# Score, projection, FFN and output products in tiles of 64x64 instead of 64x32, beside P.V in 64x32

## The chip, the cores and the metric

The kernel runs on one core of one Trainium2 chip. The metric is the device time of one execution in microseconds (us); the median of several runs counts. TensorE multiplies, VectorE (DVE), ScalarE (ACT) and GpSimd (POOL) work on the results, and SyncE (SP) issues most of the DMAs. On TensorE each product is two instructions: a load of the stationary operand (the profile calls this queue PEld) and the matmul that streams the moving operand past it (PE).

## The reference

One input `x` of 2048 tokens by 512 features goes through an attention block (32 heads of 16) and through a gated FFN of width 1376; a sigmoid gate mixes the two. All inputs are bf16.

```python
    qkv = (x @ wqkv)                       # q, k, v: 32 heads, Dh = 16
    scores = jnp.einsum("bhqd,bhkd->bhqk", q, k) * (Dh ** -0.5)
    p = _softmax(scores, axis=-1)
    o = jnp.einsum("bhqk,bhkd->bhqd", p, v)
    a = o_merged @ wo
    ...
    g_ = jnp.einsum("bsd,df->bsf", x, w_gate)
    u = jnp.einsum("bsd,df->bsf", x, w_up)
    b = jnp.einsum("bsf,fd->bsd", g_ * u, w_down)
    ...
    g = _sigmoid((x * gate_w).sum(-1, keepdims=True))
    return g * a + (1 - g) * b
```

(Names are shortened here; the shapes are those of the reference.)

## The kernel before

**Halves and tiles.** After a short prologue TensorE is used as two halves of 64 rows, `r = 0` and `r = 1`. One job is what a half does at once: a product of 64 contraction rows with up to 128 output columns and 512 moving columns, written as matmuls side by side, each at its own place in the array. `pe64` (line 1570) issues such a list; `tile_position=(64 * r, 32 * cc)` names the half and the column where a matmul's tile begins. In the kernel before, every job is four matmuls of 64 rows by 32 columns, so eight tiles cover the array when both halves work. The shape of a tile in the built program follows from the operands: rows and output columns, rounded up to 32, 64 or 128.

**Which jobs there are.** `scores` (line 1579) makes the scores of 128 keys by 512 queries for one head: the stationary operand is a slice of the keys `KT`, the moving one the masked queries `QM`. `fill` (line 1607) makes one contraction step of everything that is a plain matrix product: the k, q and v projections, the FFN's up and gate products (`u`, `g`), the FFN's down product together with the output projection (`do`), the last chunk's output projection (`fin`), and the row of the gate (one column wide). `pv` (line 1595) makes P.V: four heads in one job, each with its own 17 columns (16 of V and one of ones, which gives the softmax's denominator) and its own moving operand, so that these are four matmuls in four 32-column places by nature. `tail_out` makes the last output products, again with four matmuls a job. The only full-array matmuls are those of the prologue (7 warm-up matmuls, 16 transposes, 32 projections) and `x_turn` (line 1651), four calls of four transposes each near the beginning.

**What the other engines do.** ACT takes the exponential of part of the score tiles out of PSUM, up to three banks in one instruction. For the other part DVE forms the exponential as an integer pass over the scores' bits, and DVE and GpSimd (`int64_add`) make three shifted copies of it, which P.V then reads with scaled copies `Vs` of V. DVE also copies projections, multiplies up by gate, and scales outputs.

**What sets the order.** A planner (`_Sched`) runs when the program is built: an event loop with a clock, assumed durations (0.216 us for a job on one half), tables of limits by time, and pools of PSUM banks and SBUF cells. At each step it picks for each half the next job: P.V on one half (`vh`), scores and filling products on the other, mostly in turn. Each pick becomes one call of `scores`, `pv` or `fill`, which appends one operation to the plan; `emit` then writes each engine's list in that order and adds the semaphore waits that the operands need. An operation's wait stands at its first matmul, and its signal at its last. The number of matmuls inside a job is not known to the planner: neither the choice nor the order of jobs depends on it.

Of the kernel before, what the change touches and what calls it, by code (L numbers as in the profile page):

```python
# [1502 lines left out]
class _Hw:  # L1503
# [63 lines left out]
        self.ps = stack.enter_context(nc.psum_tensor("ps", [128, 8, 512], F32))  # L1567


    def pe64(self, r, mms, deps):  # L1570
        def fn(pe):
            o = None
            for dst, lhs, rhs, st, sp, cc in mms:
                o = pe.matmul(dst, lhs, rhs, start=st, stop=sp, tile_position=(64 * r, 32 * cc), skip_group_check=True)  # L1574
            return o

        return self.P.op("pe", fn, deps, "pe%d" % r)

    def scores(self, r, bank, c, b, s, kt, ci, deps):
        var = s + 2 * (ci % 2)  # L1580
        lo, hi = 64 * r, 64 * r + 64
        q = self.QM[lo:hi, (4 * c + b) % 2, var, :]
        mms = []
        for cc in range(4):
            k0 = kt * 128 + 32 * cc
            mms.append((self.ps[32 * cc : 32 * cc + 32, bank, :], self.KT[lo:hi, b, k0 : k0 + 32], q, True, True, cc))
        return self.pe64(r, mms, deps)

    def cell(self, x, lo, hi):
# [17 lines left out]
    def fill(self, u, r, i, start, stop, deps):  # L1607
        lo, hi = 64 * r, 64 * r + 64
        bank = u.bank
        kind = u.mm[0]  # L1610
        mms = []
        n = 4
        if kind == "gate":
            for cc in range(1, 4) if u.mm[1] else (0,):
                mms.append((self.ps[32 * cc : 32 * cc + 1, bank, :], self.gw[lo:hi, i : i + 1], self.xT[lo:hi, cc, i, :], start, stop, cc))
            return self.pe64(r, mms, deps)
        for cc in range(4):
            c0 = 32 * cc
            if kind in ("k", "q", "u", "g"):
                if kind == "k":  # L1620
                    b, ch = u.mm[1:]
                    w = self.wk[lo:hi, i, 128 * b + c0 : 128 * b + c0 + 32]
                elif kind == "q":
                    ch, b = u.mm[1:]
                    w = self.wq[lo:hi, i, 128 * b + c0 : 128 * b + c0 + 32]
                else:
                    ch, f = u.mm[1:]
                    if c0 >= self.FW[f]:
                        continue
                    w = (self.wu if kind == "u" else self.wg)[lo:hi, i, 128 * f + c0 : 128 * f + c0 + 32]  # L1630
                x = self.xT[lo:hi, ch, i, :]
            elif kind == "v":
                ch, tt = divmod(u.mm[1], 4)
                t0 = 128 * tt + c0
                w, x = self.xT[lo:hi, ch, i, t0 : t0 + 32], self.wv[lo:hi, i, :]
            elif kind == "do":
                c, tt = u.mm[1:]
                t0 = 128 * tt + c0
                if i < 11:
                    w, x = self.hT[lo:hi, i, t0 : t0 + 32], self.wd[lo:hi, i, :]  # L1640
                else:
                    w, x = self.OT[lo:hi, (4 * c + i - 11) % 8, t0 : t0 + 32], self.wo[lo:hi, i - 11, :]
            else:
                t0 = 128 * u.mm[1] + c0
                w = self.OT[lo:hi, (12 + i) % 8, t0 : t0 + 32]
                x = self.wo[lo:hi, i, :] if i < 3 else self.wq[lo:hi, 0, :]
            mms.append((self.ps[c0 : c0 + 32, bank, :], w, x, start, stop, cc))
        return self.pe64(r, mms, deps)


# [531 lines left out]
```

## Time and profile before

| | |
|---|---|
| median of 3 runs | 699.54 us |
| the runs | 699.54, 692.03, 699.86 us |
| the profiled execution | 705.51 us, span of its instructions 703.7 us |
| granted TensorE clock, mean | 0.997 |
| HBM read, written | 12.23 MB, 2.36 MB |

The page of the profile gives busy time and instruction count of each engine, the span in 40 slices, the chain of work that ended last, and the costliest groups of instructions. A row of a group names the line, the engine, the operation, output and inputs, the tile's rows and columns where it is a matmul (64*32), the operands' shapes and the count; then the busy time as a union, the mean length of one in ns, and the idle time before the group with what ended it. `issue` is time in which an engine waited for nothing that the profile shows. Lengths of matmuls are modelled; the distance between the starts of two matmuls on one tile says how long the tile is taken.

Busy time in two stretches of the span (PE, PEld, DVE, ACT, POOL in us):

| stretch | PE | PEld | DVE | ACT | POOL |
|---|---|---|---|---|---|
| 200 to 300 us | 99.24 | 58.62 | 87.95 | 98.07 | 89.96 |
| 690 to 704 us | 9.16 | 5.21 | 6.09 | 6.13 | 1.49 |

### The profile page before, as it was taken

What the parts mean: (1) busy time and instruction counts of PE and PEld (TensorE: products, weight loads), DVE (VectorE), ACT (ScalarE), POOL (GpSimd) and SP (SyncE); (2) the same over time, 40 slices, a digit from 0 to 9 for tenths busy, and PEclk for the clock granted to TensorE, in tenths of its full rate; (3) what the DMA queues carried; (4) which work ended last, traced back from release to release, by engine and by line L of the source; (5) the groups of instructions that cost most, each with busy time, mean ns of one, the idle gap of its engine ahead of it and who ended that gap; (6) DMA issues with size and microseconds to landing.
All of it is one profiled execution on the core that took longest, in us unless ns stands there. A gap on an engine that the chain in (4) does not pass through costs nothing.

```text
span 703.7 us, 49393 instructions
## 1 busy us (share of the span) xinstructions
PE 682.0 (97%) x22839; PEld 393.0 (56%) x22839; DVE 624.5 (89%) x1008; ACT 660.0 (94%) x1040; POOL 545.3 (77%) x617
## 2 busy tenths in 40 slices
PE   8999999999999999999997999999999999999997
PEld 5566555455465565555653566545554565556564
DVE  7889989899898879999998888999899878999985
ACT  5899999999899999999997999999999999999995
POOL 3455988788989889998997667879799877772790
PEclk9999999999999999999999999999999999999999
DMA  9101422001310010101010010100101010010101
GB/s 180 45 5 29 112 66 65 13 9 32 85 36 19 23 33 18 30 6 36 6 24 23 20 43 13 36 4 13 28 10 38 13 27 30 12 28 12 37 8 46
DMA packets 32126, 23.06 MB, mean 33 GB/s; under 512 B 17356, under 2 KB 28524, under 8 KB 31920
## 3 DMA queue, kind: packets, MB, share of 16 engines
q1 hardware_dynamic: 30784, 18.86, 10.6%
q8 instruction: 178, 2.92, 1.8%
q0 software_dynamic: 176, 0.53, 0.5%
q10 hardware_dynamic: 960, 0.52, 0.3%
q14 instruction: 28, 0.23, 0.1%
HBM read 12.23 MB, written 2.36 MB: 21 GB/s over the span
## 4 chain that ended last, share of the span: by engine, by line
PE 92%; DVE 4%; issue 2%; POOL 1%; ACT 0%; DVEq 0%; POOLq 0%; ACTq 0%
PE ps L1574 92%; DVE DB L1710 1%; DVE OT L1869 1%; POOL DB L1717 1%; PE ps L1978 0%; DVE io L1880 0%; ACT wu L1671 0%; PE ps L1963 0%; DVE hT L1848 0%; ACT wd L1671 0%; POOL wk L1717 0%; DVE wk L1710 0%; DVE gden L1697 0%; DVE ident L1885 0%; DVE qraw L1732 0%
## 5 line engine op out<-in xcount | busy, mean ns | idle before, releaser
L1574 PE MATMUL ps<-QM,KT 64*32 64x512 bf16 x8192 | 560.1, 379 | 6.9 <-DVE wk L1710 3.6
L1717 POOL INT64_ADD DB<-DB x402 | 362.5, 917 | 94.8 <-PE ps L1574 36.4
L1710 DVE TENSOR_SCALAR DB<-ps 128x512 int16<-128x512 f32 x595 | 391.4, 690 | 42.2 <-PE ps L1574 38.0
L1671 ACT ACTIVATE PT<-ps 128x512 bf16<-128x512 f32 (+1 forms) x574 | 376.8, 749 | 11.4 <-PE ps L1574 10.3
L1574 PE MATMUL ps<-DB,Vs 64*17 64x512 bf16 x3448 | 320.3, 377 | 2.6 <-issue 1.8
L1574 PEld LDWEIGHTS ps<-QM,KT 64*32 64x32 bf16 x8192 | 196.2, 90 | 153.0 <-DVE DB L1710 39.2
L1574 PE MATMUL ps<-PT,Vp 64*17 64x512 bf16 x1478 | 221.3, 377 | 1.5 <-issue 1.4
L1671 ACT ACTIVATE xT<-ps 128x512 bf16<-128x512 f32 (+1 forms) x288 | 205.5, 779 | 10.3 <-PE ps L1574 8.8
L1574 PE MATMUL ps<-xT,Vp 64*17 64x512 bf16 x784 | 144.2, 377 | 0.8 <-issue 0.6
L1574 PE MATMUL ps<-DB,Vp 64*17 64x512 bf16 x1200 | 123.5, 377 | 0.7 <-issue 0.6
L1574 PE MATMUL ps<-xT,wg 64*32 64x512 bf16 x1376 | 121.4, 377 | 1.1 <-ACT wd L1671 0.9
L1574 PE MATMUL ps<-xT,wu 64*32 64x512 bf16 x1376 | 120.7, 377 | 0.0
L1574 PEld LDWEIGHTS ps<-DB,Vs 64*17 64x17 bf16 x3448 | 92.2, 87 | 35.2 <-issue 8.7
L1574 PE MATMUL ps<-wd,hT 64*32 64x512 bf16 x1408 | 104.7, 380 | 0.0
L1671 ACT ACTIVATE wd<-ps 128x512 bf16<-128x512 f32 (+1 forms) x101 | 66.1, 740 | 3.4 <-PE ps L1574 2.8
L1717 POOL INT64_ADD wv<-DB x65 | 56.1, 869 | 14.1 <-PE ps L1574 8.5
L1574 PEld LDWEIGHTS ps<-PT,Vp 64*17 64x17 bf16 x1478 | 56.3, 86 | 14.3 <-issue 3.5
L1574 PEld LDWEIGHTS ps<-xT,wg 64*32 64x32 bf16 x1376 | 39.8, 92 | 17.9 <-PE ps L1574 2.2
L1574 PE MATMUL ps<-wv,Vs 64*17 64x512 bf16 x472 | 48.8, 376 | 0.0
L1717 POOL INT64_ADD DB<-wk x46 | 42.4, 936 | 7.5 <-DVE wk L1710 6.8
L1574 PEld LDWEIGHTS ps<-xT,wu 64*32 64x32 bf16 x1376 | 39.4, 92 | 15.1 <-issue 2.7
L1574 PEld LDWEIGHTS ps<-wd,hT 64*32 64x32 bf16 x1408 | 37.5, 93 | 11.2 <-issue 1.5
(115 smaller groups left out, 873.3 us busy)
## 6 DMA issues: line engine op xcount, KB each, us to landing
rb<-rscr SPq DMA_DIRECT2D x16, 256.0 KB
QM<-qraw SPq DMA_DIRECT2D x124, 16.0 KB, 2.3
oc<-oraw SPq DMA_DIRECT2D x60, 32.0 KB, 2.0
out_dram<-ost SPq DMA_DIRECT2D x12, 128.0 KB, 1.9
wd<-in_B_w_down_dram SPq DMA_DIRECT2D x10, 128.0 KB, 2.5
wu<-in_B_w_up_dram SPq DMA_DIRECT2D x12, 96.0 KB, 2.8
wg<-in_B_w_gate_dram SPq DMA_DIRECT2D x12, 96.0 KB, 2.6
OT<-in_A_x_dram SPq DMA_DIRECT2D x2, 256.0 KB, 4.5
```

What stands on the lines that cost most here:

```text
L1574: o = pe.matmul(dst, lhs, rhs, start=st, stop=sp, tile_position=(64 * r, 32 * cc), skip_group_check=True)
L1671: return self.P.op("act", lambda a: a.activation(dst, src, ACT.Exp, scale=self.ES), deps)
L1710: return self.dve(lambda v: v.tensor_scalar(dst, src, self.YB, 0.0, ALU.add, ALU.max), deps)
L1717: return self.P.op("pool", lambda e: e.int64_add(o.bitcast(I64), a.bitcast(I64), 32 * v * 0x0001000100010001), deps)
L1869: return self.dve(lambda v: v.tensor_tensor(self.OT[:, bi % 8, :], self.oc[:], self.rb[:], ALU.mult), deps)
```

## The change

The four-way loop in `scores` and in `fill` becomes a loop in steps of a width, `SW` and `PW`, both 64. Each matmul covers 64 output columns, so a job is two matmuls of 64 rows by 64 columns. Where the last FFN tile is only 96 columns wide, the second matmul is 32 wide. The gate's row, `pv`, `tail_out`, the prologue and `x_turn` are as before, and so are all waits and the order of the jobs. The lines behind the added ones move down by two.

```diff
+    SW, PW = 64, 64
+
     def pe64(self, r, mms, deps):
...
-        for cc in range(4):
-            k0 = kt * 128 + 32 * cc
-            mms.append((self.ps[32 * cc : 32 * cc + 32, bank, :], self.KT[lo:hi, b, k0 : k0 + 32], q, True, True, cc))
+        for c0 in range(0, 128, self.SW):
+            k0 = kt * 128 + c0
+            mms.append((self.ps[c0 : c0 + self.SW, bank, :], self.KT[lo:hi, b, k0 : k0 + self.SW], q, True, True, c0 // 32))
         return self.pe64(r, mms, deps)
...
-        for cc in range(4):
-            c0 = 32 * cc
+        for c0 in range(0, 128, self.PW):
+            n = self.PW
             if kind in ("k", "q", "u", "g"):
                 if kind == "k":
                     b, ch = u.mm[1:]
-                    w = self.wk[lo:hi, i, 128 * b + c0 : 128 * b + c0 + 32]
+                    w = self.wk[lo:hi, i, 128 * b + c0 : 128 * b + c0 + n]
...
                     ch, f = u.mm[1:]
-                    if c0 >= self.FW[f]:
+                    n = min(n, self.FW[f] - c0)
+                    if n <= 0:
                         continue
-                    w = (self.wu if kind == "u" else self.wg)[lo:hi, i, 128 * f + c0 : 128 * f + c0 + 32]
+                    w = (self.wu if kind == "u" else self.wg)[lo:hi, i, 128 * f + c0 : 128 * f + c0 + n]
...
                 if i < 11:
-                    w, x = self.hT[lo:hi, i, t0 : t0 + 32], self.wd[lo:hi, i, :]
+                    w, x = self.hT[lo:hi, i, t0 : t0 + n], self.wd[lo:hi, i, :]
...
-            mms.append((self.ps[c0 : c0 + 32, bank, :], w, x, start, stop, cc))
+            mms.append((self.ps[c0 : c0 + n, bank, :], w, x, start, stop, c0 // 32))
         return self.pe64(r, mms, deps)
```

More of the change, by code (lines that the diff above doesn't have):

```diff
@@ L1611, in fill @@
         mms = []
-        n = 4
         if kind == "gate":
@@ L1621, in fill @@
                     b, ch = u.mm[1:]
-                    w = self.wk[lo:hi, i, 128 * b + c0 : 128 * b + c0 + 32]
+                    w = self.wk[lo:hi, i, 128 * b + c0 : 128 * b + c0 + n]
                 elif kind == "q":
                     ch, b = u.mm[1:]
-                    w = self.wq[lo:hi, i, 128 * b + c0 : 128 * b + c0 + 32]
+                    w = self.wq[lo:hi, i, 128 * b + c0 : 128 * b + c0 + n]
                 else:
                     ch, f = u.mm[1:]
-                    if c0 >= self.FW[f]:
+                    n = min(n, self.FW[f] - c0)
+                    if n <= 0:
                         continue
-                    w = (self.wu if kind == "u" else self.wg)[lo:hi, i, 128 * f + c0 : 128 * f + c0 + 32]
+                    w = (self.wu if kind == "u" else self.wg)[lo:hi, i, 128 * f + c0 : 128 * f + c0 + n]
                 x = self.xT[lo:hi, ch, i, :]
@@ L1634, in fill @@
                 t0 = 128 * tt + c0
-                w, x = self.xT[lo:hi, ch, i, t0 : t0 + 32], self.wv[lo:hi, i, :]
+                w, x = self.xT[lo:hi, ch, i, t0 : t0 + n], self.wv[lo:hi, i, :]
             elif kind == "do":
@@ L1639, in fill @@
                 if i < 11:
-                    w, x = self.hT[lo:hi, i, t0 : t0 + 32], self.wd[lo:hi, i, :]
+                    w, x = self.hT[lo:hi, i, t0 : t0 + n], self.wd[lo:hi, i, :]
                 else:
-                    w, x = self.OT[lo:hi, (4 * c + i - 11) % 8, t0 : t0 + 32], self.wo[lo:hi, i - 11, :]
+                    w, x = self.OT[lo:hi, (4 * c + i - 11) % 8, t0 : t0 + n], self.wo[lo:hi, i - 11, :]
             else:
                 t0 = 128 * u.mm[1] + c0
-                w = self.OT[lo:hi, (12 + i) % 8, t0 : t0 + 32]
+                w = self.OT[lo:hi, (12 + i) % 8, t0 : t0 + n]
                 x = self.wo[lo:hi, i, :] if i < 3 else self.wq[lo:hi, 0, :]
-            mms.append((self.ps[c0 : c0 + 32, bank, :], w, x, start, stop, cc))
+            mms.append((self.ps[c0 : c0 + n, bank, :], w, x, start, stop, c0 // 32))
         return self.pe64(r, mms, deps)
```

## The prediction

> **What bounds the kernel now.** I read the first lines of the page, then the chain of work that ended last, then the groups by shape, and last the timeline of TensorE, once in the middle and once where it changes the shape of its tiles.
>
> ```profile
> span 703.7 us, 49393 instructions
> PE 682.0 (97%) x22839; PEld 393.0 (56%) x22839; DVE 624.5 (89%) x1008; ACT 660.0 (94%) x1040; POOL 545.3 (77%) x617
> ...
> PEclk9999999999999999999999999999999999999999
> ...
> PE 92%; DVE 4%; issue 2%; POOL 1%; ACT 0%; DVEq 0%; POOLq 0%; ACTq 0%
> ...
> L1574 PE MATMUL ps<-QM,KT 64*32 64x512 bf16 x8192 | 560.1, 379 | 6.9 <-DVE wk L1710 3.6
> L1574 PE MATMUL ps<-DB,Vs 64*17 64x512 bf16 x3448 | 320.3, 377 | 2.6 <-issue 1.8
> L1574 PE MATMUL ps<-PT,Vp 64*17 64x512 bf16 x1478 | 221.3, 377 | 1.5 <-issue 1.4
> ```
>
> TensorE carries 92% of the chain. ACT (660.0 us busy) and DVE (624.5 us) follow close behind, so today the plan of the work is balanced: a saving on TensorE alone would soon meet ACT, while a loss on TensorE has nothing that hides it. The clock row stands at 9 in every slice, so the clock is no cause of anything here. The 379 ns of one matmul is a modelled length; what a tile costs in a stream is read from starts:
>
> ```profile
> 299.99 0.39 PE L1574 MATMUL ps<-xT,wg 64*32 64x512 bf16 x4
> ...
> 300.20 0.39 PE L1574 MATMUL ps<-QM,KT 64*32 64x512 bf16 x4
> 300.25 0.39 PE L1574 MATMUL ps<-DB,Vs 64*17 64x512 bf16 x4
> 300.42 0.39 PE L1574 MATMUL ps<-xT,wg 64*32 64x512 bf16 x4
> 300.47 0.55 PE L1574 MATMUL ps<-QM,KT 64*32 64x512 bf16 x8
> 300.69 0.39 PE L1574 MATMUL ps<-DB,Vs 64*17 64x512 bf16 x4
> 300.85 0.39 PE L1574 MATMUL ps<-xT,wu 64*32 64x512 bf16 x4
> 300.90 0.39 PE L1574 MATMUL ps<-DB,Vp 64*17 64x512 bf16 x4
> 301.07 0.44 PE L1574 MATMUL ps<-QM,KT 64*32 64x512 bf16 x8
> ```
>
> The columns are start, length, engine, line and operation, tiles, count. One half of the array (64 rows) starts a job of four matmuls at 299.99, 300.20, 300.42, 300.64 (inside the eight that begin at 300.47), 300.85 and 301.07: five steps in 1.08 us, 0.216 us each. The other half does the same 0.05 us later. So eight 64x32 tiles run at once, and P.V (the 64*17 rows) on one half lies fully beside a score or a projection on the other. The program order has 22,768 tiled matmuls; an eighth of them times 0.216 is 615 us of the 703.7. What runs alongside is what makes the kernel as fast as it is.
>
> **What the change removes, adds and moves.** Counted in the order of the changed kernel, TensorE has 15,703 matmuls in place of 22,839: 14,272 of 64x32 become 7,136 of 64x64. The 8,368 of P.V (17 columns wide, placed as 64x32), the 32 of the gate, the 64 that remain in the last FFN tile of 96 columns (64 + 32) and the 32 of the tail stay 64x32. No job moves on any engine, no wait is added, none removed; the queues of DVE, ACT, GpSimd and the DMAs are the same. So the sum has three terms.
>
> First, fewer instructions. They are worth at most what TensorE loses to their supply:
>
> ```profile
> PE ps L1574 <- issue: 7.0, 18, 1.0
> ```
>
> All idle time of TensorE that waits for nothing else the profile shows is 7.0 us. A job of two starts its second matmul sooner than a job of four its fourth, but the next job on that half starts 0.216 us after the first either way, so that is worth nothing on the path. Bounds: -7 us to 0.
>
> Second, wider weight loads:
>
> ```profile
> L1574 PEld LDWEIGHTS ps<-QM,KT 64*32 64x32 bf16 x8192 | 196.2, 90 | 153.0 <-DVE DB L1710 39.2 <-ACT PT L1671 10.5 <-issue 10.0
> ...
> L1658 PEld LDWEIGHTS ps<-ident,OT 128*128 128x128 bf16 x16 | 1.0, 103 | 0.5 <-issue 0.5
> ```
>
> A load of 32 columns takes 90 ns, one of 128 columns 103 ns; one of 64 lies between, say 94 ns. It has the 216 ns of the job before to hide in, as now. If that cover went, it would be at most 0.013 us more at each job that is exposed.
>
> Third, and this decides: the stream now mixes two tile shapes. Today all of it is 64x32, except for four transposes of the input early on, in 128x128:
>
> ```profile
> 11.15 0.10 PEld L1574 LDWEIGHTS ps<-QM,KT 64*32 64x32 bf16 x4 [0.37 <-DVE KT L1993]
> 11.48 0.50 PEld L1658 LDWEIGHTS ps<-ident,OT 128*128 128x128 bf16 x8 [0.23 <-issue]
> ...
> 12.64 0.23 PEld L1658 LDWEIGHTS ps<-ident,OT 128*128 128x128 bf16 x4 [0.23 <-issue]
> 12.97 0.12 PEld L1574 LDWEIGHTS ps<-QM,KT 64*32 64x32 bf16 x8
> ```
>
> ```profile
> 12.30 0.41 PE L1574 MATMUL ps<-QM,KT 64*32 64x512 bf16 x8
> 12.64 0.40 PE L1658 MATMUL ps<-ident,OT 128*128 128x128 bf16 x4
> 12.97 0.61 PE L1574 MATMUL ps<-QM,KT 64*32 64x512 bf16 x8
> ```
>
> Eight score matmuls start within 0.03 us (0.41 less the 0.38 of one), the last at about 12.32 or 12.33. The transposes' first load and first matmul both come at 12.64, 0.31 to 0.32 us after that. The four scores that loaded at 11.15 to 11.16 give the same: the next shape loads at 11.48, 0.32 us later. Neither hold has a releaser but "issue". Two things are to be seen. A change of shape costs 0.32 us from the last start, against 0.216 us within one shape, so some 0.10 us is spent on emptying the array. And the load, which in the stream runs a whole job ahead of its matmul, is held too. On the way back, 12.64 plus 0.40 less the 0.22 of one short matmul puts the last transpose at 12.82, and scores follow at 12.97: 0.15 us, which is the 0.055 us step of a 128-column transpose plus the same 0.10.
>
> The trace has no change from 64x32 to 64x64. Its cost lies between 0 (the two shapes overlap as the jobs do now) and these 0.32 us with no overlap at all; a gain is excluded, since a wider tile still streams 512 columns and keeps its step. I take 0.32, the nearest row there is: what was held there was everything, on both halves, until the old shape was out.
>
> [...]
>
> Now the count. In the changed order P.V and the other work take turns:
>
> ```
> 4000 L1576 Matmult ps<-xT,wu 64x512 x2
> 4001 L1576 Matmult ps<-QM,KT 64x512 x2
> 4002 L1576 Matmult ps<-DB,Vs 17x512 x4
> 4003 L1576 Matmult ps<-QM,KT 64x512 x4
> 4004 L1576 Matmult ps<-xT,wq 64x512 x2
> 4005 L1576 Matmult ps<-xT,Vp 17x512
> 4006 L1576 Matmult ps<-PT,Vp 17x512 x3
> 4007 L1576 Matmult ps<-xT,wq 64x512 x2
> ```
>
> (place in the order, line, output and inputs, output's shape, count.) The shape changes 4,036 times. The sum on TensorE: 4,036 changes x 0.32 = 1,291 us; inside the stretches of one shape a tile comes up again 881 times, x 0.216 = 190 us; the small steps between the starts of the matmuls of a stretch (0.03 us over eight, so some 3.5 ns each), taken over all stretches, 29 us. Together 1,510 us.
>
> Around it stands what TensorE does not fill: the span begins with loads, and ends after TensorE:
>
> ```profile
> 10.31 0.41 PE L1658 MATMUL ps<-ident,OT 128*128 128x128 bf16 x4
> 10.65 0.89 PE L1574 MATMUL ps<-QM,KT 64*32 64x512 bf16 x16
> ...
> 697.51 1.90 PE L1574 MATMUL ps<-wq,OT 64*32 64x512 bf16 x36
> ```
>
> The transposes begin at 10.31 us, and the 55 full-array matmuls ahead of them account for some 4 us of that, so 6 us are added; from 699.41 to 703.7 are 4.3 us more. The other gaps of today (703.7 less 615 and these 10, some 79 us) are mostly meetings with ACT and DVE. ACT's 660 us are then 43% of the span, so little of this is left; I take 0, and keep 60 us for the upper end. Span: 1,520 us. The profiled execution took 705.51 us for a span of 703.7, 1.8 us more, and the median of the runs is 699.54, 0.8% less than the profiled one. Between these corrections I stay at **1,520 us**.
>
> The price's own uncertainty: with waiting but no 0.10 us of emptying it is 0.216 per change, and the same sum gives about 1,100 us; with half of the emptying, 1,300. Upwards, 0.013 us of longer load at every change are 52 us, and with 60 us of gaps kept, 1,630. The likeliest case's own range is 1,280 to 1,640.
>
> **The rivals.** *The shape is kept by each half.* Then a P.V job on one half and a 64x64 job on the other still run together, and only a half that goes from one to the other waits. In the order that happens 1,274 times. Each time the half loses 0.10 us, and as TensorE starts its matmuls in order, the other half is held with it: 1,274 x 0.10 = 127 us, on 699.5 about 825 us; where it falls into gaps that are there already, 790. [...] Against it: the transposes held both halves, though a 128-row tile had to.
>
> *Width does not count at all*, the side that isn't slower. In the rows quoted both the number of rows and of columns change; here the rows stay 64 and only the columns go from 32 to 64. If a hold comes from the rows alone, each 64x64 tile is just two neighbouring strips, the stream keeps its 0.216 us steps, and what is left is the first term: 699.5 less 0 to 7, so 693 to 700 us, 696 in the middle. It decides the whole outcome from the first P.V job on: the 300.42 pair above would look the same with x2 and x4. For it: the start spacing shows that tiles with their own weights run side by side. Against it: the 0.10 us of emptying, which no sharing of rows explains, since a tile followed by one of its own shape needs none. [...]
>
> That the change does not do what it says is excluded: the built program carries 7,136 matmuls with 64 columns.
>
> **How the numbers follow.** Full hold at each change: 0.75. Hold by half: 0.08. No hold: 0.17. Faster by over 2% (2% is about what a measurement of this kernel can tell from no change, its three runs lie 1.1% apart) needs more than 14 us, twice the whole issue term, so 0.03 of the last case; 0.12 of it is within 2%; 0.02 goes to a small loss from loads. Slower: 0.75 + 0.08 + 0.02 = 0.85. The own range of the first case holds some 0.7 of all; to reach 8 in 10 the range goes down over the middle prices to the case of the halves, 790, and up to 1,640.
>
> **What would show it.** In the profile after: the first P.V job beside a 64*64 job. If the full hold is right, the starts of P.V rows and 64*64 rows alternate 0.32 us apart, a load never comes ahead of its own shape's turn, TensorE's chain share goes above 95%, and ACT and DVE fall under half of the span with unchanged busy times of about 660 and 625 us. If starts of the two shapes still lie 0.05 us apart, the forecast is wrong and the no-hold rival right; if they lie together except where one half changes, it is the halves. A step of 0.216 in place of 0.32 would say that only the emptying was over-priced.

## The result and the profile after

The changed kernel takes 2,508.93 us (median of 4 runs, 2,482.46 to 2,533.60) against 698.97 us before: 3.56 times as long, 95% interval 3.52 to 3.60. (The ratio takes the two faster of the four runs, 2,482.46 and 2,489.58 us; the medians alone give 3.59.) The forecast was 1,520 us, in a range of 790 to 1,640. The direction is right, the size is not.

The first lines of the page of the changed kernel, its clock row, its chain and two groups (columns as before):

```profile
span 2487.7 us, 35121 instructions
PE 2480.6 (100%) x15703; PEld 527.2 (21%) x15703; DVE 658.5 (26%) x1008; ACT 737.2 (30%) x1040; POOL 546.1 (22%) x617
...
PEclk9655555655555555555556555555555555755555
...
PE 99%; DVE 0%; ACT 0%; issue 0%; DVEq 0%; ACTq 0%
...
L1576 PE MATMUL ps<-QM,KT 64*64 64x512 bf16 x4096 | 996.3, 606 | 0.4 <-ACT wu L1673 0.3
...
L1576 PE MATMUL ps<-DB,Vs 64*17 64x512 bf16 x3448 | 502.1, 575 | 0.0
```

Two things are to be seen. TensorE is the whole chain, 99%, and ACT and DVE have fallen to 30% and 26% of the span. And the clock row, 9 in every slice before, now reads 5 nearly everywhere: the granted clock is 0.535 in the mean. A matmul of 64x64 is modelled at 606 ns, where one of 64x32 stood at 379.

The timeline of TensorE in the changed kernel, early, while the clock is still full:

```profile
30.21 0.38 PE L1576 MATMUL ps<-xT,wk 64*64 64x512 bf16 x2
30.52 0.39 PE L1576 MATMUL ps<-DB,Vs 64*17 64x512 bf16 x4
30.84 0.40 PE L1576 MATMUL ps<-xT,wk 64*64 64x512 bf16 x2
30.85 0.40 PE L1576 MATMUL ps<-QM,KT 64*64 64x512 bf16 x2
31.08 0.38 PE L1576 MATMUL ps<-xT,wk 64*64 64x512 bf16 x2
31.09 0.38 PE L1576 MATMUL ps<-QM,KT 64*64 64x512 bf16 x2
31.30 0.38 PE L1576 MATMUL ps<-xT,wk 64*64 64x512 bf16 x2
31.61 0.39 PE L1576 MATMUL ps<-DB,Vs 64*17 64x512 bf16 x4
31.93 0.40 PE L1576 MATMUL ps<-wv,xT 64*64 64x512 bf16 x2
```

and later, with the clock at half:

```profile
1000.34 0.64 PE L1576 MATMUL ps<-xT,wu 64*64 64x512 bf16 x2
1000.35 0.64 PE L1576 MATMUL ps<-QM,KT 64*64 64x512 bf16 x2
1000.77 0.64 PE L1576 MATMUL ps<-xT,wu 64*64 64x512 bf16 x2
...
1001.87 0.64 PE L1576 MATMUL ps<-xT,wg 64*64 64x512 bf16 x2
1002.44 0.60 PE L1576 MATMUL ps<-DB,Vs 64*17 64x512 bf16 x4
1002.97 0.64 PE L1576 MATMUL ps<-QM,KT 64*64 64x512 bf16 x2
1003.54 0.60 PE L1576 MATMUL ps<-wk,Vs 64*17 64x512 bf16 x4
1004.07 0.64 PE L1576 MATMUL ps<-QM,KT 64*64 64x512 bf16 x2
```

In the first, two 64*64 jobs on the two halves still start 0.01 us apart (30.84 and 30.85), but P.V never starts beside one: 30.21 to 30.52 and 31.30 to 31.61 are 0.31 us, 30.52 to 30.84 and 31.61 to 31.93 are 0.32 us. That is the price the prediction took from the transposes. In the second the same alternation takes 0.57 us from a 64*64 job to P.V and 0.53 us back, 0.55 in the mean, and two jobs on the same tile are 0.43 us apart (1000.34 to 1000.77) instead of 0.216. The stretches (busy us and count of each engine, then the granted clock) say when it goes over:

```profile
18.00:80.00 62.00, 62.00 (x746) 19.82 (x738) 35.70 (x67) 38.74 (x62) 19.77 (x26) 1.00 0.04 12
80.00:460.00 380.00, 380.00 (x2278) 77.06 (x2274) 96.39 (x145) 103.70 (x143) 78.74 (x83) 0.50 0.05 13
460.00:473.00 13.00, 13.00 (x142) 3.86 (x140) 6.20 (x10) 6.61 (x10) 5.67 (x9) 1.00 0.11 31
473.00:1176.00 703.00, 703.00 (x4208) 143.92 (x4204) 172.68 (x253) 197.11 (x293) 159.36 (x186) 0.50 0.03 7
```

12.0 matmuls per us at full clock (746 in 62), 6.0 at half (2,278 in 380). With the mean of 0.535, some 7% of the span is at full clock, 174 us. The measured prices give the span back: at half clock throughout, 4,036 changes x 0.55 and 881 repeats x 0.43, with the 29 us of start spacing, are 2,628 us; the 174 us at full clock do what takes 174 x 2,628 / 1,510 = 303 us at half; 2,628 - 303 + 174 is 2,499 us, against 2,487.7 (the 10 us or so at the two ends are not in the sum).

### The profile page after: what moved, and what is told of

The parts are those of the page before. It is cut to its first block, busy times and chain, and to the rows that moved or that the text cites. A ratio compares the mean times of both kernels' runs of the same rounds, so it can differ in the third digit from the quotient of the medians.

```text
span 2487.7 us, 35121 instructions
## 1 busy us (share of the span) xinstructions
PE 2480.6 (100%) x15703; PEld 527.2 (21%) x15703; DVE 658.5 (26%) x1008; ACT 737.2 (30%) x1040; POOL 546.1 (22%) x617
## 4 chain that ended last, share of the span: by engine, by line
PE 99%; DVE 0%; ACT 0%; issue 0%; DVEq 0%; ACTq 0%
PE ps L1576 99%; DVE io L1882 0%; PE ps L1980 0%; PE ps L1965 0%; DVE hT L1850 0%; ACT wu L1673 0%; DVE ident L1887 0%; PE ps L1660 0%; ACT QM L1993 0%; DVEq L87 0%; DVE hT L1847 0%; ACT QM L1994 0%; DVE PT L1909 0%; DVE io L1883 0%; DVE ident L1879 0%
## 5 line engine op out<-in xcount | busy, mean ns | idle before, releaser
L1576 PE MATMUL ps<-QM,KT 64*64 64x512 bf16 x4096 | 996.3, 606 | 0.4 <-ACT wu L1673 0.3
L1673 ACT ACTIVATE PT<-ps 128x512 bf16<-128x512 f32 (+1 forms) x574 | 407.0, 719 | 974.8 <-PE ps L1576 974.3
L1576 PE MATMUL ps<-DB,Vs 64*17 64x512 bf16 x3448 | 502.1, 575 | 0.0
L1576 PE MATMUL ps<-PT,Vp 64*17 64x512 bf16 x1478 | 336.3, 581 | 0.1
L1576 PEld LDWEIGHTS ps<-QM,KT 64*64 64x64 bf16 x4096 | 204.8, 128 | 499.5 <-issue 437.3
L1576 PE MATMUL ps<-xT,wu 64*64 64x512 bf16 x704 | 223.8, 616 | 0.0
L1576 PE MATMUL ps<-xT,wg 64*64 64x512 bf16 x704 | 223.1, 613 | 0.0
L1576 PE MATMUL ps<-xT,Vp 64*17 64x512 bf16 x784 | 223.0, 579 | 0.0
L1576 PE MATMUL ps<-wd,hT 64*64 64x512 bf16 x704 | 200.7, 618 | 0.0
L1576 PE MATMUL ps<-DB,Vp 64*17 64x512 bf16 x1200 | 176.1, 577 | 0.1
L1576 PEld LDWEIGHTS ps<-xT,wu 64*64 64x64 bf16 x704 | 48.4, 131 | 122.1 <-issue 113.3
```

The costliest lines, as they stand in the source:

```text
L1673: return self.P.op("act", lambda a: a.activation(dst, src, ACT.Exp, scale=self.ES), deps)
```

## The experiments

Theory A: a change of tile shape empties the array, and the clock falls because too little of the array then streams, whatever leaves it idle. Theory B: tiles of 64 columns are themselves slow. Theory C: the changes of shape lower the clock, not the idle time that they make. Where nothing else is said, a time is that of one profiled execution, with the kernel before beside it on the same chip (691.91 us for the first four kernels, 698.27 for the next four).

### All tiles 64x64, and waits in place of changes

In the first, P.V is two wide tiles as well:

```diff
...
         mms = []
-        for cc in range(4):
...
-            mms.append((self.ps[32 * cc : 32 * cc + 17, 7, :], w, self.cell(cells[cc], lo, hi), first, True, cc))
-        return self.pe64(r, mms, deps)
+        for cc in (0, 2):
+            w = self.w1[lo:hi, :]
+            mms.append((self.ps[32 * cc : 32 * cc + 64, 7, :], w, self.cell(cells[cc], lo, hi), first, True, cc))
+        return self.pe64(r, mms, list(deps) + [self.r["w1"]])
...
```

> P.V too is issued as two 64x64 tiles a job, with a constant tile of ones as stationary operand and the moving operand of two of its four heads; the other two heads and the values of V are left out. Nearly the whole stream then has one shape (162 changes of shape are left, from the gate row and the 96-column FFN tile, against 4,036). Theory A (a change of shape empties the array, and TensorE's clock falls because the array then streams too small a share of the time): the hold is gone, starts of the two halves overlap again, TensorE's own sum is 673 us, the whole some 740 us, clock near 1. Theory B (the 64-column tiles themselves are slow, by their wider load or by their place in the array): no better than 2,500 us, since all tiles are then 64 columns wide.

Measured: 706.26 us, clock 0.999. Its timeline:

```profile
300.19 0.42 PE L1577 MATMUL ps<-QM,KT 64*64 64x512 bf16 x4
300.41 0.38 PE L1577 MATMUL ps<-xT,wu 64*64 64x512 bf16 x2
300.45 0.38 PE L1577 MATMUL ps<-wv,w 64*64 64x512 bf16 x2
300.62 0.38 PE L1577 MATMUL ps<-QM,KT 64*64 64x512 bf16 x2
300.67 0.38 PE L1577 MATMUL ps<-DB,w 64*64 64x512 bf16 x2
300.84 0.38 PE L1577 MATMUL ps<-QM,KT 64*64 64x512 bf16 x2
```

P.V (300.45, 300.67) again starts 0.04 to 0.05 us after the other half's job, and each half steps by 0.21 to 0.22 us. Theory B falls: with every tile wide the kernel is within 2.1% of the one before. This kernel has 11,519 matmuls, half of before, and is no faster. That does not measure the first term of the prediction's sum, though: 162 changes of shape are left in it, and at some 0.2 us each they can hide a gain of 7 us. Its list of waits has no row of `issue` any more, and neither has that of the changed kernel.

The second keeps 64x32 everywhere and adds a wait where the order goes from P.V to another kind of job or back:

```diff
-        return self.P.op("pe", fn, deps, "pe%d" % r)
+        wide = mms[0][1].shape[-1] == 32
+        last = getattr(self, "pelast", None)
+        if last is not None and last[0] != wide:
+            deps = list(deps) + [last[1]]
+        o = self.P.op("pe", fn, deps, "pe%d" % r)
+        self.pelast = (wide, o)
+        return o
```

> The kernel before, all tiles 64x32, with one thing added: wherever the order goes from P.V to another kind of job or back, the first matmul waits by semaphore until the job before it is complete. So there are no changes of shape, but 3,960 waits at nearly the places of the 4,036 changes. Theory A: the clock falls here too, since the array streams 0.21 us of every 0.43; at full clock the sum of TensorE would be 1,940 us, at half clock 2,990 us, and I expect a mean clock below 0.6 and 2,800 to 3,050 us. Theory C (the change of shape itself lowers the clock, not the idle time it makes): the clock stays near 1 and the time is about 1,950 us.

Measured: 3,066.36 us, clock 0.513. Two stretches:

```profile
20.00:46.00 26.00, 23.10 (x436) 7.19 (x428) 13.69 (x25) 12.84 (x21) 6.31 (x7) 1.00 0.03 8
46.00:1060.00 1014.00, 918.41 (x7428) 155.67 (x7428) 215.80 (x329) 241.55 (x345) 184.15 (x216) 0.50 0.03 9
```

Without any change of shape in these stretches the clock goes to half at 46 us, and later it comes back only for moments. The time lies a little above the 2,800 to 3,050 us expected. Theory C falls: no change of shape is needed. What is left is that little of the array streams, for a part of the time none of it, since a job here waits for the one before it, and otherwise mostly one half. Which of the two counts, this run alone does not say.

### Wide tiles in a part of the jobs

```diff
-    SW, PW = 64, 64
+    SW, PW = 64, 32
```

> Only the scores are 64x64; projections, FFN and output products go back to 64x32. The shape changes 3,078 times instead of 4,036. TensorE's sum is 1,230 us at full clock and 2,160 us at half. Theory A: 0.31 to 0.33 us per change where the clock is full and 0.52 to 0.56 us where it is half; the array streams somewhat more of the time than in the changed kernel (73% of it at full clock against 71%), so the clock is a little higher than 0.535 in the mean, 0.55 to 0.65, and the time is 1,900 to 2,150 us. Theory B: by the number of wide tiles (4,096 of 7,136) 57% of the loss, 1,730 us.

```diff
-    SW, PW = 64, 64
+    SW, PW = 32, 64
```

> Only projections, FFN and output products are 64x64; the scores go back to 64x32. The shape changes 2,817 times. TensorE's sum is 1,230 us at full clock and 2,180 us at half. Theory A: close to the run with wide scores alone, although it has 3,040 wide matmuls and that one 4,096: 1,850 to 2,150 us, clock 0.55 to 0.7. Theory B: by the number of wide tiles 43% of the loss, 1,470 us.

Measured: 1,485.59 us with wide scores alone (clock 0.823), 1,602.61 us with wide filling products alone (0.750). Both expectations of theory A were too slow, by more than 400 and 240 us: the clock held up much better than I thought. Theory B's are missed too: by the number of wide tiles the first should be the slower one. (One execution of each; how far executions of such a kernel lie apart is shown further below, so their order says no more than that.)

Then two that choose the kind of job:

```diff
-    SW, PW = 64, 64
+    SW, PW = 32, 64
...
-        for c0 in range(0, 128, self.PW):
-            n = self.PW
+        pw = 64 if kind in ('k', 'q', 'v') else 32
+        for c0 in range(0, 128, pw):
+            n = pw
```

> Only the k, q and v projections are 64x64, everything else 64x32: 631 changes of shape. TensorE's sum at full clock, by 0.31 to 0.33 us per change with no overlap across it, is 770 us against 639 for the kernel before. With few changes the array stays busy enough for the full clock (theory A): clock above 0.97 and, with the prediction's price, 770 us plus up to the 65 us of gaps of the kernel before: 790 to 850 us. If a few changes are enough to lower the clock, above 900 us.

and the same with `('u', 'g')`:

> Only the FFN's up and gate products are 64x64: 1,323 changes of shape. TensorE's sum is 916 us at full clock. Theory A: the clock holds for most of the span, 0.9 or more, and the time is 930 to 1,080 us; the more changes there are in a stretch, the more the clock falls, so the three runs with 1,323, 2,817 and 4,036 changes should not lie on a line from the kernel before.

Measured: 869.09 us (clock 0.916) and 983.84 us (clock 0.967). The second is as expected. The first is slower than expected, and its stretches show where:

```profile
5.00:38.00 33.00, 31.97 (x416) 12.16 (x416) 20.05 (x38) 19.05 (x31) 7.09 (x9) 1.00 0.48 95
38.00:181.00 143.00, 143.00 (x1078) 30.47 (x1083) 36.55 (x65) 42.45 (x65) 21.25 (x29) 0.50 0.01 2
182.00:860.00 678.00, 674.16 (x20545) 348.44 (x20531) 560.40 (x884) 605.11 (x939) 512.86 (x570) 1.00 0.10 27
```

The clock goes to half at 38 us, stays there for 143 us, and is full from 182 us on, at 30 matmuls per us. The number of changes does not decide this: 285 of the 631 lie ahead of 182 us and the other 346 behind it, all of these at full clock. Nor does their density alone: there are 2.5 per us in the 18 us ahead of the fall, and 2.4 per us from 20 to 120 us in the run with wide scores alone, where the clock stays full. What differs is how much streams between them: by the share that the next part works out, 0.43 of the array ahead of the fall here (0.31 in the last 3.41 us), 0.48 there. Per change, over the kernel before on the same chip, the loss was 0.27 us with 631 changes (869.09 - 698.27), 0.22 us with 1,323 (983.84 - 698.27), 0.32 us with 2,817 (1,602.61 - 691.91), 0.26 us with 3,078 (1,485.59 - 691.91) and 0.45 us with 4,036 (2,508.93 - 698.97): no straight line, and no order by number either. At full clock the sums give 0.21 us (916 less 639, over 1,323 changes): a job that had half of 0.216 us, sharing the array, has 0.32 us to itself. I put what is above that down to the clock.

### What the clock follows

P.V twice in a row, and one 64x128 tile in place of two 64x64:

```diff
+        mms += [x[:3] + (False,) + x[4:] for x in mms]
         return self.pe64(r, mms, deps)
```

> The changed kernel with each P.V matmul issued twice in a row into the same place, so that numerator and denominator both double and their ratio stays. The 4,036 changes of shape stay; the array streams longer between them. TensorE's sum is 1,940 us at full clock, 3,480 us at half. Theory A1 (the clock follows the share of the array's cells that stream): that share is 0.43 at full clock, as good as the 0.41 of the changed kernel, because P.V streams on one half alone; so the clock stays low, 0.52 to 0.6 in the mean, and the time is 3,100 to 3,450 us. Theory A2 (it follows the share of time in which any tile streams): that share rises from 0.71 to 0.78, above the runs with wide scores alone or wide filling products alone (0.73 and 0.75, clocks 0.823 and 0.750), so the clock is above 0.8 and the time 2,000 to 2,400 us.

```diff
-    SW, PW = 64, 64
+    SW, PW = 128, 128
```

> The wide products as one tile of 64x128 a job instead of two of 64x64; P.V stays 64x32. The shape changes 3,988 times. If the price is one emptying of the array per change, whatever the widths, nothing moves: TensorE's sum is 1,470 us at full clock and 2,560 at half (changed kernel: 1,490 and 2,590), the clock is about 0.53, the time 2,400 to 2,560 us. If the price grows with the width (longer load, more columns to empty), each change costs 0.02 to 0.05 us more and the time is 2,600 us or above.

Measured: 3,278.22 us, clock 0.545, and 2,410.74 us, clock 0.537. The first is theory A1's, and not A2's with its clock above 0.8: more streaming of P.V, on its one half, did not bring the clock back. The second lies below the 2,508.93 us of the changed kernel, in the 2,400 to 2,560 us expected for a price that does not grow with the width.

From the records of ten of these traces (before, changed, and the eight kernels above) I worked out, for each 3.41 us, which share of the array's eight 64x32 places streams: for each matmul that starts in the stretch, its places times 512 columns at the granted clock (steps of 0.216 us at full clock and 0.43 us at half, above), over eight places and 3.41 us. The length is that of the trace's own clock records: the times between two changes of the clock are its multiples (13.653 us from 459.691 to 473.344 in the changed kernel). Counted by share, rounded to 0.05:

```
share          stretches at full clock, of them the last before half    at half clock, last before full
0.00 to 0.30           23, 18                                                343, 0
0.35 and 0.40         206, 26                                                798, 0
0.45 to 0.65          692, 0                                                2279, 0
0.70                   33, 0                                                  50, 7
0.75                   24, 0                                                  26, 6
0.80 to 1.00          599, 0                                                  31, 30
```

(The counts move by a few per cent with where the first stretch is laid.) In these traces the clock fell only out of stretches with 0.40 or less, and returned only out of stretches with 0.70 or more. Between the two, at 0.45 to 0.65, it stayed as it was. A low share did not bring it down at once: 44 of the 229 stretches with 0.40 or less at full clock are the last before half. Nearly every job here covers all 128 columns of its half, so places and rows of the array cannot be told apart. In the run with wide scores alone this can be seen side by side:

```profile
204.00:300.00 96.00, 96.00 (x1536) 28.14 (x1532) 54.31 (x84) 59.10 (x83) 43.98 (x48) 1.00 0.05 9
...
510.00:660.00 150.00, 150.00 (x1190) 28.88 (x1186) 43.90 (x63) 48.06 (x78) 40.75 (x44) 0.50 0.02 5
```

16.0 matmuls per us at full clock and 7.9 at half: in clock periods the same density, at either clock. If that is so, chance decides how long it stays at each, and executions should lie far apart:

> The kernel with wide scores alone once more, several executions. If the clock has two thresholds, so that a stretch in which about half of the array's cells stream keeps whichever clock it came in with, small shifts in time decide when the clock falls or comes back, and the executions should lie far apart: 1,350 to 1,700 us, several per cent between them, where the kernel before spreads by 1%. If the clock simply follows the momentary share, all executions lie within 1% of 1,486 us.

> The kernel with wide k, q and v projections alone once more. With two thresholds, the full clock should come back in some executions earlier than at the 182 us of the first look or not fall at all: times from 780 us (clock full throughout) to 870 us. If the clock follows the momentary share, all lie within 1% of 869 us.

Measured: six executions with wide scores alone took 1,468.91, 1,486.26, 1,533.40, 1,567.36, 1,573.79 and 1,630.33 us, 11% from the fastest to the slowest, beside 0.8% of the kernel before (687.30 to 692.64). Their mean clocks run from 0.833 to 0.732 in the same order. That is what the expectation has for two thresholds. The two traces of this kernel (on two chips) show it job by job: 3,222 of its 18,743 matmuls, by their place in the order, ran at full clock in one execution and at half in the other. With wide projections alone, four executions took 854.16 to 871.91 us, 2%, and none kept the full clock (0.916 to 0.929 in the mean): this one decides nothing, since its clock falls in every execution, and none came near the 780 us of a clock that stays full. The traces of both runs keep to the bounds of the table.

None of these kernels is faster than the one before.

## Why the prediction was wrong, point by point

- *First, fewer instructions, -7 us to 0.* Not measured. The row of `issue` with its 7.0 us is gone after the change, but nothing of it could show beside the loss, and the kernel with half the matmuls (706.26 us) has changes of shape left.
- *Second, wider loads, hidden.* Right for a stream of one shape, as the all-64x64 kernel shows: a load takes 105 ns there, a little over the 94 estimated, and the halves still step by 0.21 to 0.22 us.
- *I take 0.32, the nearest row there is.* Right: where the clock is full, 0.33 us in the median into P.V and 0.31 us out of it, for both halves. The price for two widths that share the 64 rows is the one seen for 128x128 against 64x32.
- *4,036 changes, 881 repeats.* Right: the trace of the changed kernel has the 4,036 too, and with the measured prices the two give the span to within 1%.
- *The shape is kept by each half.* Refuted: P.V on one half and a 64*64 job on the other never start together; at full clock the trace has no change between 64*64 and P.V with less than 0.30 us between the two starts. What this rival's sum took as given, that TensorE starts its matmuls in order, the trace bears out: 99% of the 15,703 stand at their place in the order of the program.
- *Width does not count at all.* Refuted by the same rows. Tiles overlap within one shape, as the 0.01 us between 30.84 and 30.85 shows, and not across two.
- *Between these corrections I stay at 1,520 us.* The step that failed lies ahead of it: "The clock row stands at 9 in every slice, so the clock is no cause of anything here." That row told of a kernel whose array was nearly always full: 615 us of full streaming in 703.7, a share of 0.87. The working itself had P.V stream alone on one half for 0.216 us of each 0.32, which is a third of the array's places, and over the whole sum 615 us of full streaming in 1,510, a share of 0.41; I took the clock of the full array for an array at such a load. The 0.216 and the 0.32 were right for the first 80 us, and 0.43 and 0.55 for nearly all the rest.
- *ACT and DVE under half of the span with unchanged busy times.* The shares are right (30%, 26%). The busy times are not: DVE rose from 624.5 to 658.5 us and ACT from 660.0 to 737.2. ACT's operations did not grow longer: the 574 exponentials of PT were 749 ns in the mean and are 719 after, together 430 and 413 us. Yet their busy time went from 376.8 to 407.0 us, because before many of them overlapped and now hardly any do.

So the hold of 0.31 to 0.33 us and the count of 4,036 stood, and the loss beyond the forecast, some 990 us, is the clock, by the sum above. That the clock falls without any change of shape when little of the array streams is shown by the kernel with waits in place of changes (0.513 in the mean), and that wide tiles alone leave it full by the kernel with all tiles 64x64 (0.999). That it follows the share of places, with a lower bound (0.40) and an upper one (0.70), rests on the counts above and on the spread of the executions; what exactly is counted there, places, rows or something else, and where the bounds lie to better than 0.05, stays open.

In all clock records of the changed kernel the granted clock is 1.0 or 0.5, and idle gaps of TensorE do not explain the 0.5: its list of waits has no row above 1.2 us:

```profile
PE ps L1956 <- DVE io L1878: 1.2, 1, 1.2
PE ps L1965 <- DVE ident L1887: 0.8, 1, 0.8
PE ps L1576 <- ACT wu L1673: 0.3, 1, 0.3
```

With a busy row of 100%, the clock still fell where 0.40 or less of the array's places streamed.

## What to carry to other kernels

Keep one tile shape in any stretch where products of different kinds are to run side by side; a wider tile in some of them cost the overlap here and about 0.1 us at each change (0.31 to 0.33 us in place of 0.216), and if the widest common shape is 64x32, use it for all. When a change leaves TensorE busy but with fewer of its places filled, price every step at half clock as well (0.55 us in place of 0.32 here) and carry that as a case of its own, with the share of places as its condition (0.40 or less here). Compare such kernels over several executions, because in the middle of the range (a share of 0.45 to 0.65 here) the clock kept its past.

## What the runs showed of the hardware that I had not expected

The clock had a memory here: at a share of 0.45 to 0.65, 692 stretches at full clock and 2,279 at half all went on as they were, so one kernel took 1,469 us and 1,630 us on the same chip. And PE's busy share tells nothing of it: it read 97% in the kernel before and 100% in the one that takes 3.56 times as long.
